# Search rounds ahead of the first expert, and weight conversions ahead of their gather, in an attention, feed-forward and routed-experts kernel

## The chip, the core and the metric

The kernel runs on one core of a Trainium2 chip. The metric is the device time of one execution in microseconds (us); lower is better. The core's engines work side by side, each through its own list of instructions in order: PE multiplies matrices, DVE, ACT and POOL work on elements, SP issues most transfers, and POOL also issues the transfers whose rows are picked by an index.

## The reference

Three parts follow one another: causal attention with a memory term over 4 x 8 heads, 576 positions of 64; a feed-forward layer with squared ReLU over the 2304 resulting tokens of 512 numbers; and a layer of eight experts, with 288 tokens each, cut here to what matters:

```python
def _moe2_ref(x, w_gate, w1, w2):
    N, D = x.shape
    E = w_gate.shape[1]
    cap = N // E
    logits = x @ w_gate
    flat = logits.flatten()
    order = np.argsort(-flat)
    ...
    for idx in order:
        tok, e = (int(idx) // E, int(idx) % E)
        if assigned[tok] >= 0 or counts[e] >= cap:
            continue
        assigned[tok] = e
        counts[e] += 1
    ...
    for e in range(E):
        mask = assigned == e
        h = np.maximum(x[mask] @ w1[e], 0.0)
        out[mask] = h @ w2[e]
```

All token and expert pairs are taken in order of falling score, and each pair whose token is free and whose expert has room is joined. Each expert then multiplies its own 288 tokens by its two weight matrices.

## The kernel before

Attention and the feed-forward layer take the first 740 us and are the same in both kernels. The change lies in the last stage, class `Moe`.

**Routing.** The greedy join is done in phases (`phase`). A phase finds the expert that fills next, by a search for a threshold: `search` is called twice, on the upper and the lower 16 bits of the scores, and does three rounds each. A round is a comparison on DVE (`cmp`), 18 small counting matmuls on PE (`rs<-hot,cmp`), a comparison on DVE (`fl`), one matmul that spreads the answer (`rs<-fl,jo`), and a sum on DVE (`nb`). So a phase has six rounds, then a count (`gm`) and a prefix sum over tokens (`ab`, `prefix`), after which the expert's number is known (`number`, tile `ei`). `lists` then turns the members into three lists of 96 token numbers (18 small matmuls `rs<-rhs,oh`, tile `idx`).

**An expert's data.** `load` brings its weights in four transfers of 1 MB into `wraw` (three buffers), issued by SP once the number is known. `gather` brings its 288 rows by three transfers that POOL issues (`xg`). `convert` splits each loaded part into a high and a low half (`wsp`, six buffers): two activations on ACT, then two subtractions on POOL. In the kernel before, the conversion stands inside `lists`, behind the gather.

**An expert's products.** `head` transposes the gathered rows on PE and splits them (`xs`); `hidden` does 8 blocks of 12 products (`ph<-xs,wsp`) with results to `hs`; `output` 4 blocks of 24 (`ph<-hs,wsp`) with results to `yt`; `tail` transposes back and POOL stores the rows. An expert has 192 products.

**The order on PE** is written out by `run`: every yield of `mlps` is one product or transpose, every yield of `routes` one step of the routing, and the number that the step yields says how many products go by before the next step. `LEAD` is the number of routing steps that stand ahead of the first expert (two steps a round). A factor of 0.75 cuts short waits while fewer experts are ready than `AHEAD` allows. `EARLY` is the number of experts whose list is finished at once, not in pieces beside the next phase's search.

**The order on the other engines** (ACT, DVE, POOL, SP) is chosen by the framework's scheduler when the kernel is built, from the dependences and its own model of durations; `issue_after` adds an order between two engines' instructions. In the built program each engine keeps that order strictly.

Of the kernel before, what the change touches and what calls it, by code (L numbers as in the profile page):

```python
# [383 lines left out]
def run(work):  # L384

    while True:
        try:
            next(work)
        except StopIteration as e:
            return e.value  # L390


class Ffn:
# [123 lines left out]
    def later(self, gpool, beside, turn):  # L517
# [12 lines left out]
        def hide(n, c):  # L530
            last = n == len(steps) - 1 and c != PASSES[-1][0]
            G[n][c] = run(self.hidden(xs[n], c, self.gb if last else gpool))

        get(0)
        for n, (p, i) in enumerate(steps):
# [41 lines left out]
            for d in range(KD):  # L577
                py = self.p2x.tile([128, 512], F32, name="py")[:, 0:TW]
                run(self.output(py, G[n], cs, d))
                nc.vector.tensor_tensor(y[:, d], py, y[:, d], op=OP.add)  # L580
            if not final:
                nc.sync.dma_start(self.yp_d[1][i].rearrange("(k p) t -> p k t", p=128), self.Y.pop(i))
            else:
                after = [lambda i=i: run(self.logits(i)), lambda i=i: run(self.rows(i))]
# [82 lines left out]
NE = 8  # L667
# [7 lines left out]
NEVER = 1 << 30  # L675
CUTS = (2, 2, 2, 2)
ON_DVE = ()
LEAD = 6
GAPS = (60, 12, 12, 15, 12, 12, 12, 18, 48, 6)
AHEAD = 3  # L680
EARLY = 2


class Moe:
# [116 lines left out]
    def t18(self, nm, dt=F32):  # L801
        return self.rt.tile([128, NTT], dt, name=nm)
# [149 lines left out]
    def lists(self, i, raws):  # L952

        nc, V, two, t18 = self.nc, self.nc.vector, self.rt, self.t18
        yield "v"
        j, r, pos, rb, jh = t18("j"), t18("r"), self.pos, self.rb, self.jh
        V.tensor_scalar(j, pos, float(CW), None, op0=OP.is_ge)
        V.scalar_tensor_tensor(j, pos, float(2 * CW), j, op0=OP.is_ge, op1=OP.add)
        V.scalar_tensor_tensor(r, j, -float(CW), pos, op0=OP.mult, op1=OP.add)
        V.scalar_tensor_tensor(rb, r, 1.0, self.mem, op0=OP.add, op1=OP.mult)  # L960
        V.tensor_tensor(jh, j[:, :, None].to_broadcast([128, NTT, 3]),
                        self.j3p[:, None, :].to_broadcast([128, NTT, 3]), op=OP.is_equal)
        rhs = two.tile([128, NTT, 3, 2], BF16, name="rhs")
        V.tensor_tensor(rhs, jh[:, :, :, None].to_broadcast([128, NTT, 3, 2]),
                        self.tp[:, :, None, :].to_broadcast([128, NTT, 3, 2]), op=OP.mult)
        oh = two.tile([128, NTT, CW], BF16, name="oh")
        n = NTT // CUTS[3]
        for t0 in range(0, NTT, n):
            yield "v"
            V.tensor_tensor(oh[:, t0:t0 + n], rb[:, t0:t0 + n, None].to_broadcast([128, n, CW]),  # L970
                            self.slot[:, None, :].to_broadcast([128, n, CW]), op=OP.is_equal)
        yield "p"
        ps = self.p1.tile([CW, 3, 2], F32, name="rs")
        for t in range(NTT):
            nc.tensor.matmul(ps.rearrange("p a b -> p (a b)"), oh[:, t], rhs[:, t].rearrange("p a b -> p (a b)"),
                             start=(t == 0), stop=(t == NTT - 1))
        yield "v"
        V.tensor_reduce(self.idf[0:CW], ps, axis=mybir.AxisListType.X, op=OP.add)
        idx = self.ri.tile([CW, 3], I32, name="idx")
        V.tensor_copy(idx, self.idf[0:CW])  # L980
        self.ready.append((self.split[i], idx, self.gather(idx)))
        with self.tc.issue_after(self.got):
            self.convert(i, raws if i else raws[:1])
        if i == 0:
            self.raws = raws[1:]

    def number(self):
# [4 lines left out]
    def routes(self):  # L992

        self.beside = self.wants = None
        for i in range(NE):
            if i < NE - 1:
                yield from self.phase()
            else:
                yield from self.finish()
                yield from self.rest()  # L1000
            er = self.number()
            if i == 0:
                self.settle()
            raws, self.split[i] = self.load(er), []
            self.beside = self.lists(i, raws)
            self.wants = next(self.beside)
            if i < EARLY or i == NE - 1:
                yield from self.finish()

    def finish(self):  # L1010
# [93 lines left out]
    def mlps(self, routes):  # L1104

        yield from self.head(0, range(KD))
        with self.tc.issue_after(self.last):
            self.convert(0, self.raws)
        for i in range(NE):
            for f in range(KE):  # L1110
                yield from self.hidden(i, f)
                if 1 <= f <= 3 and i:
                    yield from self.tail(i - 1, [f - 1])
            for d in range(KD - 1):
                yield from self.output(i, d)
            work = self.output(i, KD - 1)
            if i + 1 < NE:
                while len(self.ready) <= i + 1:
                    next(routes, None)
                for k in range(0, KD, 2):  # L1120
                    yield from self.head(i + 1, [k, k + 1])
                    for _ in range(KE * 3 // 2 if k == 0 else 0):
                        next(work)
                        yield
            yield from work
            self.done = i + 1
        yield from self.tail(NE - 1, range(3))

    def run(self, close, other, settle):

        self.settle = settle
        with self.tc.manual_schedule(engines={mybir.EngineType.PE}):
            routes, wait = self.routes(), 0
            owed = 0
            close()
            while not self.ready:
                owed += min(0.6 * next(routes, 0), 24)
                while owed > 0:
                    owed -= next(other, NEVER)
            for _ in range(LEAD):  # L1140
                wait = next(routes)
            for _ in self.mlps(routes):
                wait -= 1
                if wait <= 0 and len(self.ready) <= self.done + AHEAD:
                    wait = next(routes, NEVER)
                    if len(self.ready) < self.done + AHEAD and wait <= 15:
                        wait *= 0.75


@with_exitstack  # L1150
# [126 lines left out]
```

## Time and profile before

| | us |
|---|---|
| median of 3 runs | 1064.56 |
| the three runs | 1064.21 to 1068.12 |
| the profiled execution | 1064.33 |
| its span in the profile | 1062.6 |
| PE busy (91% of the span) | 970.3 |
| DVE, ACT, POOL busy | 666.0, 554.7, 526.0 |

The span runs from the first to the last instruction; the execution's own time has 1.7 us around it. A busy share is an average over the whole kernel. What the change is worth is to be read from the stage of the experts alone, and there from what PE waits for, and from the clock that PE is granted (PEclk, 1.00 is 2.4 GHz and 0.50 is 1.2 GHz).

### The profile page before, as it was taken

The numbers are of one execution on the slowest core, as the hardware profiler recorded it, in microseconds if no ns is written. First come the engines' busy times: TensorE is split into PE (matmuls) and PEld (weight loads), VectorE is DVE, ScalarE is ACT, GpSimd is POOL, SyncE is SP. The second block draws the span as 40 slices with busy tenths as digits, with TensorE's granted clock in tenths as the row PEclk, the third lists the DMA queues.
The fourth block names the chain that finished last, engine by engine and source line by source line (L and its number), as shares of the span: only waits on it lengthen the run. The fifth ranks groups of instructions, "written<-read, shape, count | busy, mean of one in ns | idle before, by whom it ended". The sixth has DMA issues, their size and how long they took to land.

```text
span 1062.6 us, 19791 instructions
## 1 busy us (share of the span) xinstructions
PE 970.3 (91%) x7017; PEld 886.8 (83%) x7017; DVE 666.0 (63%) x1966; ACT 554.7 (52%) x1370; POOL 526.0 (50%) x503
## 2 busy tenths in 40 slices
PE   4677799999999988999999999998789989999996
PEld 3555588989898988999999999875688888889996
DVE  7998878888888737256428932336557567773110
ACT  6776878888888745344323333521442334344531
POOL 3665666566656525345212111211763637878841
PEclk9767899999999999999999999999689689999999
DMA  6453455464636277679573333002452345445501
GB/s 149 121 152 101 113 148 157 94 171 110 179 75 166 63 231 234 209 252 312 184 265 107 119 120 120 30 21 72 150 181 91 114 156 181 156 145 180 192 26 30
DMA packets 150723, 150.75 MB, mean 142 GB/s; under 512 B 71640, under 2 KB 122840, under 8 KB 150496
## 3 DMA queue, kind: packets, MB, share of 16 engines
q1 hardware_dynamic: 147552, 140.05, 43.2%
q0 software_dynamic: 3072, 9.44, 2.9%
q8 instruction: 55, 0.90, 0.3%
q14 instruction: 44, 0.36, 0.1%
HBM read 111.69 MB, written 37.77 MB: 141 GB/s over the span
## 4 chain that ended last, share of the span: by engine, by line
PE 61%; DVE 13%; issue 9%; ACT 7%; DMA 6%; POOL 3%; SPq 2%; POOLq 0%; ACTq 0%; DVEq 0%
PE ph L1053 12%; PE ph L44 7%; PE ph L45 6%; PE ph L46 6%; PE py L44 4%; PE py L45 4%; PE py L46 4%; PE ps L312 3%; ACT P L240 2%; PE ps L217 2%; PE ps L271 2%; DMA xg<-y_d,idx 2%; PE rs L832 2%; DMA wraw<-in_moe_w_dram 2%; DVE ptb L26 1%
## 5 line engine op out<-in xcount | busy, mean ns | idle before, releaser
L477 POOL TENSOR_TENSOR gf<-r 128x384 f32<-128x384 f32 (+1 forms) x108 | 87.0, 806 | 206.6 <-ACT r L475 198.3
L1037 POOL TENSOR_TENSOR wsp<-wraw,wsp 128x1024 fp32r<-128x1024 f32 x64 | 150.5, 2383 | 11.9 <-ACT wsp L1035 11.6
L1053 PE MATMUL ph<-hs,wsp 128*128 128x288 f32 x768 | 124.9, 317 | 0.9 <-DVE hs L1077 0.9
L1053 PE MATMUL ph<-xs,wsp 128*128 128x288 f32 x768 | 121.5, 308 | 0.0
L26 DVE TENSOR_TENSOR gs<-gf,gs 128x384 fp32r<-128x384 f32 (+1 forms) x108 | 63.7, 590 | 91.5 <-ACT gs L25 90.9
L1053 PEld LDWEIGHTS ph<-hs,wsp 128*128 128x128 f32 x768 | 112.1, 201 | 2.8 <-DVE hs L1077 1.6
L246 POOL TENSOR_SCALAR P<-P,R,og 128x128 f32<-128x128 f32 (+2 forms) x144 | 94.7, 671 | 34.1 <-DVE R L244 14.7
L1053 PEld LDWEIGHTS ph<-xs,wsp 128*128 128x128 f32 x768 | 107.8, 193 | 1.2 <-issue 0.5
L475 ACT ACTIVATE r<-ph 128x384 f32<-128x384 f32 (+1 forms) x108 | 48.6, 450 | 75.6 <-PE ph L46 74.4
L1035 ACT ACTIVATE wsp<-wraw 128x1024 fp32r<-128x1024 f32 x64 | 64.1, 1051 | 44.1 <-DMA wraw<-in_moe_w_dram 28.6
L240 ACT ACTIVATE P<-P,R 128x128 f32<-128x128 f32 (+2 forms) x144 | 83.2, 579 | 6.8 <-POOL P L246 2.7
L25 ACT ACTIVATE gs<-gf 128x384 fp32r<-128x384 f32 (+1 forms) x108 | 52.5, 486 | 56.2 <-POOL gf L477 48.0
L44 PE MATMUL ph<-xt,win 128*128 128x384 f32 x240 | 81.3, 339 | 0.0
L45 PE MATMUL ph<-xt,win 128*128 128x384 f32 x240 | 80.9, 337 | 0.0
L46 PE MATMUL ph<-xt,win 128*128 128x384 f32 x240 | 80.7, 336 | 0.0
L271 PE MATMUL ps<-ident,P 128*128 128x128 f32 x320 | 62.2, 302 | 12.0 <-POOL P L246 4.9
L44 PE MATMUL ph<-xs,win 128*128 128x288 f32 x192 | 63.5, 331 | 3.9 <-ACT yo L514 2.6
L45 PE MATMUL py<-gs,wout 128*128 128x384 f32 x192 | 64.6, 337 | 0.0
L217 PE MATMUL ps<-kt,qt 64*128 64x128 f32 (+3 forms) x384 | 55.8, 386 | 9.4 <-DVE kt L26 3.5
L26 DVE TENSOR_TENSOR ptb<-ps,ptb 128x256 fp32r<-128x256 f32 (+3 forms) x128 | 59.6, 467 | 7.3 <-ACT ptb L25 5.7
L46 PE MATMUL py<-gs,wout 128*128 128x384 f32 x192 | 63.9, 336 | 0.0
L44 PE MATMUL py<-gs,wout 128*128 128x384 f32 x192 | 63.4, 338 | 0.0
(259 smaller groups left out, 2610.6 us busy)
## 6 DMA issues: line engine op xcount, KB each, us to landing
wraw<-in_moe_w_dram SPq DMA_DIRECT2D x32, 1024.0 KB, 5.4
xt<-xs_d SPq DMA_DIRECT2D x12, 1536.0 KB, 7.7
x_d<-xo SPq DMA_DIRECT2D x32, 288.0 KB, 3.9
xf<-x_d SPq DMA_DIRECT2D x32, 288.0 KB, 3.5
xs_d<-xs SPq DMA_DIRECT2D x8, 1152.0 KB, 5.9
raw<-in_moe_w_in_dram SPq DMA_DIRECT2D x16, 512.0 KB, 4.2
raw<-in_moe_w_out_dram SPq DMA_DIRECT2D x16, 512.0 KB, 4.4
yp<-yo SPq DMA_DIRECT2D x32, 144.0 KB, 3.6
```

Source lines behind the costliest of these rows:

```text
L26: (eng or nc.vector).tensor_tensor(lo, src, hi.bitcast(F32), op=OP.subtract)
L44: nc.tensor.matmul(out, lhi, rhi, start=start, stop=False)
L45: nc.tensor.matmul(out, lhi, rlo, start=False, stop=False)
L46: nc.tensor.matmul(out, llo, rhi, start=False, stop=stop)
L217: nc.tensor.matmul(ps[j][:, 0:w], qt[r0, a, qs], kt[r0, b, 0:w], start=i == 0, stop=i == 2)
L240: nc.scalar.activation(pw, pw, AF.Exp, bias=R[:, 0, u:u + 1], scale=-1.0, accum_out=R[:, 1, u:u + 1])
L246: nc.gpsimd.tensor_scalar(PP[n][w], PP[n][w], R[:, 2, w:w + 1], og9[:, hp, w:w + 1], op0=OP.mult, op1=OP.mult)
L271: nc.tensor.transpose(tr[:, 128 * i:128 * i + 128], P[:, 128 * i:128 * i + 128], ident)
L477: nc.gpsimd.tensor_tensor(gf, r, r, op=OP.mult)
L1035: nc.scalar.activation(w[:, 0, hs], raw[:, hs], AF.Copy)
L1037: eng.tensor_tensor(w[:, 1, hs], raw[:, hs], w[:, 0, hs].bitcast(F32), op=OP.subtract)
L1053: nc.tensor.matmul(out, l[a], r[b], start=i + p == 0, stop=i == n - 1 and p == 2)
```

## The change

Four edits go together. `LEAD` is 12, so that six rounds of the second phase's search stand ahead of expert 0, not three. The weights of experts 1 to 7 are converted where they are loaded, ahead of their list and gather. Expert 1's list is no longer finished at once. The factor of 0.75 is gone.

```diff
--- before.py
+++ after.py
@@ -675,10 +675,9 @@
 NEVER = 1 << 30
 CUTS = (2, 2, 2, 2)
 ON_DVE = ()
-LEAD = 6
+LEAD = 12
 GAPS = (60, 12, 12, 15, 12, 12, 12, 18, 48, 6)
 AHEAD = 3
-EARLY = 2
 
 
 class Moe:
@@ -979,9 +978,9 @@
         idx = self.ri.tile([CW, 3], I32, name="idx")
         V.tensor_copy(idx, self.idf[0:CW])
         self.ready.append((self.split[i], idx, self.gather(idx)))
-        with self.tc.issue_after(self.got):
-            self.convert(i, raws if i else raws[:1])
         if i == 0:
+            with self.tc.issue_after(self.got):
+                self.convert(i, raws[:1])
             self.raws = raws[1:]
 
     def number(self):
@@ -1002,9 +1001,11 @@
             if i == 0:
                 self.settle()
             raws, self.split[i] = self.load(er), []
+            if i:
+                self.convert(i, raws)
             self.beside = self.lists(i, raws)
             self.wants = next(self.beside)
-            if i < EARLY or i == NE - 1:
+            if i in (0, NE - 1):
                 yield from self.finish()
 
     def finish(self):
@@ -1143,8 +1144,6 @@
                 wait -= 1
                 if wait <= 0 and len(self.ready) <= self.done + AHEAD:
                     wait = next(routes, NEVER)
-                    if len(self.ready) < self.done + AHEAD and wait <= 15:
-                        wait *= 0.75
 
 
 @with_exitstack
```

Where it moves instructions. First POOL, from the gather of expert 0 on (`xg` is a gather, `wsp` a conversion, two for each of an expert's four parts, `out_dram` a store). The kernel before:

```order
L1044 DMA xg<-y_d,idx 96x512 x3
L1037 TENSOR_TENSOR wsp<-wraw,wsp 128x1024 x8
L1044 DMA xg<-y_d,idx 96x512 x3
L1037 TENSOR_TENSOR wsp<-wraw,wsp 128x1024 x8
L1098 DMA out_dram<-yo,idx 2304x512 x3
L1044 DMA xg<-y_d,idx 96x512 x3
L1037 TENSOR_TENSOR wsp<-wraw,wsp 128x1024 x8
```

The changed kernel:

```order
L1045 DMA xg<-y_d,idx 96x512 x3
L1038 TENSOR_TENSOR wsp<-wraw,wsp 128x1024 x14
L1045 DMA xg<-y_d,idx 96x512 x3
L1038 TENSOR_TENSOR wsp<-wraw,wsp 128x1024 x2
L1099 DMA out_dram<-yo,idx 2304x512 x3
L1038 TENSOR_TENSOR wsp<-wraw,wsp 128x1024 x6
L1045 DMA xg<-y_d,idx 96x512 x3
```

Expert 1's gather, the second one, stood behind the eight conversions of expert 0; it now stands behind these and six of its own. Expert 2's stands behind six of its own too.

Then PE, at the end of the last round ahead of expert 0 (`tr<-ident,xg` are the transposes of expert 0, `ph<-xs,wsp` its products). The kernel before:

```order
L832 MATMUL rs<-hot,cmp 32x8
L837 LDWEIGHTS jo_1_94
L837 MATMUL rs<-fl,jo_1_94 128x8
L1065 MATMUL tr<-ident,xg 128x96 x12
L1053 MATMUL ph<-xs,wsp 128x288 x3
L832 LDWEIGHTS cmp
L832 MATMUL rs<-hot,cmp 64x8
```

The changed kernel:

```order
L831 MATMUL rs<-hot,cmp 32x8
L836 LDWEIGHTS jo_1_111
L836 MATMUL rs<-fl,jo_1_111 128x8
L1066 MATMUL tr<-ident,xg 128x96 x12
L883 LDWEIGHTS ones
L883 MATMUL rs<-gm,ones 128x288
L1054 MATMUL ph<-xs,wsp 128x288 x18
```

Before, a round follows after three products; now the search is over ahead of the transposes (its last round is the one of `jo_1_111`), and the count `gm` follows them.

Last ACT, from the last block of expert 0's hidden layer before, and from its fifth in the changed kernel (`hs` reads a block of the hidden layer, `wsp` are the conversions of expert 1's weights, `yt` reads a block of the output). The kernel before:

```order
L1076 ACTIVATE hs_9856<-ph 128x288
L1035 ACTIVATE wsp<-wraw 128x1024 x2
L1086 ACTIVATE yt<-ph 128x288
L1035 ACTIVATE wsp<-wraw 128x1024 x2
L1086 ACTIVATE yt<-ph 128x288
L1035 ACTIVATE wsp<-wraw 128x1024 x2
L1086 ACTIVATE yt<-ph 128x288
L25 ACTIVATE xs<-tr 128x288 x2
L1035 ACTIVATE wsp<-wraw 128x1024 x2
```

The changed kernel:

```order
L1077 ACTIVATE hs_9848<-ph 128x288
L1036 ACTIVATE wsp<-wraw 128x1024 x2
L1077 ACTIVATE hs_9864<-ph 128x288
L1077 ACTIVATE hs_9910<-ph 128x288
L1036 ACTIVATE wsp<-wraw 128x1024 x2
L1077 ACTIVATE hs_9947<-ph 128x288
L1036 ACTIVATE wsp<-wraw 128x1024 x2
L1087 ACTIVATE yt<-ph 128x288
L1036 ACTIVATE wsp<-wraw 128x1024 x2
L1087 ACTIVATE yt<-ph 128x288 x2
```

The first conversions of expert 1 stood behind all eight `hs`; they now stand ahead of the sixth.

## Rows read from the trace of the kernel before

**Rows 1.** The profile's page: its first line.
```profile
span 1062.6 us, 19791 instructions
```

**Rows 2.** Stretches, experts 0 to 5: length; engines' busy time (count); PEclk; DMA share; GB/s.
```profile
755.80:799.40 43.60, 40.33 (x342) 36.45 (x340) 23.01 (x88) 19.89 (x31) 32.77 (x16) 0.85 0.33 112
799.40:847.20 47.80, 45.57 (x409) 40.79 (x410) 30.47 (x114) 14.25 (x25) 20.49 (x14) 0.82 0.35 114
847.20:889.60 42.40, 39.09 (x356) 36.20 (x356) 28.04 (x115) 17.39 (x29) 25.28 (x15) 0.92 0.38 128
889.60:930.70 41.10, 38.58 (x391) 34.82 (x391) 32.16 (x124) 17.49 (x29) 29.96 (x17) 1.00 0.56 194
930.70:969.20 38.50, 37.04 (x354) 34.80 (x353) 24.69 (x94) 15.36 (x27) 28.75 (x18) 0.96 0.54 172
969.20:997.40 28.20, 28.20 (x218) 27.97 (x218) 4.93 (x12) 14.56 (x25) 23.76 (x15) 1.00 0.57 180
```

**Rows 3.** Timeline of PE in experts 1 and 2: one round; one list.
```profile
822.97 0.18 PE L837 MATMUL rs<-fl,jo 64*128 64x8 bf16 x1
823.07 1.47 PE L1053 MATMUL ph<-hs,wsp 128*128 128x288 f32 x9
824.47 0.61 PE L832 MATMUL rs<-hot,cmp 128*32 128x8 bf16 x18
825.01 0.93 PE L1053 MATMUL ph<-hs,wsp 128*128 128x288 f32 x5
...
870.55 0.93 PE L975 MATMUL rs<-rhs,oh 128*96 128x6 bf16 x18 [1.51 <-DVE nb L841]
```

**Rows 4.** Timeline of DVE ahead of expert 0: where four rounds begin.
```profile
744.62 1.41 DVE L823 SCALAR_TENSOR_TENSOR cmp<-bank,jt 128x576 bf16<-128x576 int32 x2
...
747.39 0.94 DVE L823 SCALAR_TENSOR_TENSOR cmp<-bank,nb,jt 128x288 bf16<-128x288 int32 x2
...
749.44 0.94 DVE L823 SCALAR_TENSOR_TENSOR cmp<-bank,nb,jt 128x288 bf16<-128x288 int32 x2
...
751.77 1.42 DVE L823 SCALAR_TENSOR_TENSOR cmp<-bank,jt 128x576 bf16<-128x576 f32 x2
```

**Rows 5.** Timeline of PE: expert 0's transposes wait, then its first products.
```profile
753.48 0.90 PE L1065 MATMUL tr<-ident,xg 96*128 96x96 f32 x4 [1.72 <-DMA xg<-y_d,idx]
...
755.83 1.07 PE L1053 MATMUL ph<-xs,wsp 128*128 128x288 f32 x3
```

**Rows 6.** Timeline of POOL: conversions of expert 0, gathers of experts 1 and 2.
```profile
757.59 14.09 POOL L1037 TENSOR_TENSOR wsp<-wraw,wsp 128x1024 fp32r<-128x1024 f32 x6 [6.48 <-ACT wsp L1035]
...
782.53 0.92 POOL L1044 DMA_INDIRECT xg<-y_d,idx  x1 [0.30 <-issue]
...
831.61 0.94 POOL L1044 DMA_INDIRECT xg<-y_d,idx  x1 [18.82 <-DVE idx L980]
...
834.09 0.92 POOL L1044 DMA_INDIRECT xg<-y_d,idx  x1 [0.30 <-issue]
```

**Rows 7.** Timeline of PE: the transposes that follow the last gathered third.
```profile
789.83 0.42 PE L1065 MATMUL tr<-ident,xg 96*128 96x96 f32 x1 [0.53 <-DMA xg<-y_d,idx]
...
837.12 0.90 PE L1065 MATMUL tr<-ident,xg 96*128 96x96 f32 x4 [0.62 <-DMA xg<-y_d,idx]
```

**Rows 8.** Timelines of PE, DVE, SP, ACT: from prefix to conversion, expert 2.
```profile
812.68 0.18 PE L938 MATMUL rs<-ab,tri 128*128 128x36 bf16 x1
...
816.27 0.15 DVE L989 TENSOR_SCALAR ei<-bank 128x1 int32<-128x1 f32 x1
...
817.24 1.60 SPq L1025 DMA_DIRECT2D wraw<-in_moe_w_dram  x3
...
822.41 2.01 ACT L1035 ACTIVATE wsp<-wraw 128x1024 fp32r<-128x1024 f32 x2 [0.94 <-DMA wraw<-in_moe_w_dram]
```

**Rows 9.** Two stretches of expert 1, columns as in the stretches above.
```profile
829.00:832.00 3.00, 2.81 (x28) 2.81 (x28) 2.13 (x7) 0.79 (x1) 0.39 (x1) 0.73 0.00 0
...
844.00:847.00 3.00, 3.00 (x15) 2.71 (x13) 1.37 (x7) 0.00 (x0) 3.00 (x3) 0.50 0.08 25
```

## The prediction

> **What bounds the kernel now.** I read the page first, then the stretches by expert, then the timelines where PE stands or its clock is low, last POOL's and ACT's queues. The sum is made against the profiled execution, 1064.3 us, which is a span of 1062.6 [rows 1] and 1.7 around it; it lies 0.2 below the median of the runs shown. Everything ahead of the experts is the same, so only the last 310 us count.
>
> In expert 5 nothing is searched any more: 28.2 us at full clock, PE busy throughout [rows 2]. That is the price of an expert on PE, for 192 products and 24 transposes, so about 0.134 us a product if a transpose takes 0.1. Experts 0 to 4 take 43.6, 47.8, 42.4, 41.1 and 38.5 us [rows 2]. How much of that is routing? From one spreading matmul to the products after the next count, 2.04 us pass with nine products in them, then five products take 0.93 [rows 3]: 2.97 us for 14 products that cost 1.88 alone, so a round costs PE 1.1 us. A list costs 0.93 and a wait for DVE, 1.51 in a bad case [rows 3]; I take 1.2. Count and prefix I take at 0.5 an expert, an estimate. I counted the routing in the built order of before: 6, 9, 6, 7 and 5 rounds in experts 0 to 4, one list in each and three in expert 4. What an expert should take, and what it loses beyond that:
>
> - expert 0 (no tail, 1.3 less): 26.9 + 6.6 + 1.7 = 35.2, loses 8.4
> - expert 1: 28.2 + 9.9 + 1.7 = 39.8, loses 8.0
> - expert 2: 28.2 + 6.6 + 1.7 = 36.5, loses 5.9
> - expert 3: 28.2 + 7.7 + 1.7 = 37.6, loses 3.5
> - expert 4: 28.2 + 5.5 + 3.6 + 0.5 = 37.8, loses 0.7
>
> So 26.5 us are lost, 22.3 of them in the first three experts, and their granted clock is 0.85, 0.82 and 0.92 where the others have 1.00 and 0.96 [rows 2]. That loss, not the count of rounds, is what the change can touch. In expert 1 the clock falls during 829 to 832 (a mean of 0.73 puts the fall at 830.4) and is at half at 844 to 847 [rows 9], and in it stands a wait for gathered rows [rows 7]: the list came late, POOL stood idle 18.8 us for it and issued the gather at 831.6 [rows 6].
>
> **The change, part by part.**
>
> *Three rounds move ahead of expert 0.* There they hide behind nothing but the gather. On DVE a round of 64 steps takes 2.77 us, one of 32 steps 2.05, and the fourth begins at 751.8 [rows 4]; so the sixth ends at 751.8 + 2.77 + 2 x 2.05 = 758.6. Before, the transposes waited for the gather until 753.5 and the first product came 2.35 later [rows 5]. Now the gather has landed and the transposes start whole, which I put at 0.6 more: first product at 758.6 + 0.6 + 2.35 = 761.5, so **5.7 us later**. Bounds: 4 (rounds run as fast as the spacing allows while DVE splits wait) to 7 (all of the three rounds, 6.9).
>
> *Expert 1's gather stands behind twelve conversions.* Six conversions take 14.1 us on POOL and began at 757.6 [rows 6], after expert 0's last transposes; now 757.6 + 5.7 = 763.3. Six of expert 1 follow, their weights loaded meanwhile: 763.3 + 28.2 = 791.5. Three gathers are issued over 2.5 us [rows 6], and the last third lands 3.0 later when no load is in flight (issued 834.1, used 837.1), but 7.3 later when loads run beside it (782.5 to 789.8) [rows 6, 7]. Expert 1's last load is queued behind its first conversion and should have landed by then, so I take 3.0: 791.5 + 0.2 + 2.5 + 3.0 = 797.2; the other end is 801.5. PE gets there by 789.8 + 5.7 + 2.2 for two rounds more = 797.7 had it not waited before, so it waits 2 us or less more than it did. From the last third to expert 1 before took 799.4 - 789.8 = 9.6 with three rounds in it; one remains: 7.4. **Expert 1 starts at 804.6, which is 5.2 us late.**
>
> *Expert 1 gets six rounds for nine, and its list stands late in the first half.* Expert 2's number is known early: its prefix is now a few products into expert 1. From there: 3.6 us on DVE to the number, 1.0 to the load, 5.2 to the conversion on ACT [rows 8], 1 for its first half, 14.1 for six conversions, then 2.7 and 3.0 for the gather [rows 6, 7]: 30.6 us. PE reaches the transposes of expert 2 about 5 us before the end of an expert of 38.6 us, so 33 us after that prefix. The gather is in time by 2 us; that is all the margin there is. Then the late gather and the low clock after it go. I do not let the whole loss vanish: where the clock was nearly full, experts 3 and 4 still lost 3.5 and 0.7, mean 2.1. So expert 1 takes 36.5 + 2.1 = 38.6, **-9.2**.
>
> *Experts 2 to 5.* Expert 2 keeps six rounds: 38.6, **-3.8**. Expert 3 gets eight for seven: 28.2 + 8.8 + 1.7 + 2.1 = 40.8, **-0.3**. Expert 4 gets four for five and two lists for three; its 0.7 stays: 36.2, **-2.3**. Expert 5 gets a list: **+1.2**. Experts 6 and 7 are unchanged.
>
> *Conversions ahead on ACT* cost nothing in the sum: they are the same 64 activations. But an activation that waits for its load holds the `hs` behind it, DVE waits for that `hs` and PE for DVE. Four PSUM buffers of results, 12 products each, cover about 6 us of it. That is in the 2.1 us. *The dropped factor* sets 6 and 12 products between steps for 5 and 9, which gives each round's chain more cover; below zero it can cost only rounds that slip into later experts, and these are counted above.
>
> Sum: 5.2 - 9.2 - 3.8 - 0.3 - 2.3 + 1.2 = -9.2, so 1064.3 - 9.2 = **1055.1**.
>
> One rule of the Trainium skill sizes the largest term otherwise. By the rows expert 1 loses 8.0 us in all, its waits for rows included. The Trainium skill, "TensorE: Matmul & The Clock Gate", section "Terms", prices a throttled stretch at its length times one less the granted share. By that the 17 us from 830.4 to 847.2 would cost 8.4 without the waits, and expert 1 would come out some 2 us shorter than I say. The measured loss is the smaller, and I go by it.
>
> **The rivals.**
>
> *The late gather comes back at each expert (slower).* The chain of 30.6 us from prefix to gathered rows is now in front of PE for experts 2 and 3 too, since on POOL the gather cannot start before six conversions. If it runs over by more than the 2 us of margin, PE waits, the clock falls and an expert loses 8.4, as expert 0 does, not 2.1. For it: loads that meet a gather take 7.3 us where 3.0 is the rule [rows 6, 7]; ACT is more often held. Against it: expert 3's and 4's prefixes come half an expert earlier. With experts 1, 2 and 3 hit: 1055.1 + 3 x 6.3 = 1074; from two on it is no gain.
>
> *The clock falls anyway (no change).* It fell in expert 1 at 830.4, ahead of the wait for rows, with PE between rounds and a list [rows 9]. The rounds stay. If one such stretch stays, some 7 us are back: 1062.
>
> *Nearly all loss goes.* If experts 1 to 3 lose 0.7 as expert 4 does: 1055.1 - 3 x 1.4 = 1051; with the page's price of the low clock, 1049.
>
> That the change would not do what it says is excluded by the built order, where the rounds and conversions stand as described.
>
> **How the numbers follow.** A difference of 0.5%, 5.3 us, is about what a measurement of this kernel can tell from no change. Forecast 0.48, its own range 1050 to 1060 (bounds of the lead-in and of the gather's landing); nearly all goes 0.12; the clock falls anyway 0.24; late gathers 0.16. The first two are faster: 0.60; same 0.24; slower 0.16. The range reaches from the best case, 1047, to 1069, where one or two late gathers end; beyond lie most of the slower case and little below.
>
> **What would show it.** First product of expert 0 near 761.5; expert 1's gather issued near 792 with twelve conversions ahead of it; expert 1 starting near 805 and taking under 40 us with PEclk 1.00 in its second half; expert 2 starting near 843, ahead of 847.2. Wrong if PE waits for gathered rows at the end of expert 1 or 2, or if ACT's conversions wait for loads while `hs` stands behind them and the lists slip; then experts 1 to 3 take over 42 us each.

## The result and the profile after

Four executions of the changed kernel took 1050.7 to 1053.66 us, median 1052.03; four of the kernel before 1064.21 to 1071.71, median 1066.34. The ratio is 0.9856, with a 95% interval of 0.9827 to 0.9886: faster by 1.4%. The forecast was 1055.1 in a range of 1047 to 1069, and faster was its likeliest case. The profiled execution took 1052.92 us, 11.4 below that of before; the medians lie 14.3 apart. In a second comparison, with other runs of the kernel before, the same kernel had a ratio of 0.9884 (0.984 to 0.9928), where 0.983 to 0.989 was expected.

The first line of the changed kernel's page, to lay beside [rows 1]:

```profile
span 1051.2 us, 19788 instructions
```

The stretches of experts 0 to 5 in the changed kernel, with the columns of [rows 2]:

```profile
761.40:804.80 43.40, 39.76 (x341) 36.57 (x340) 25.95 (x101) 19.56 (x31) 35.66 (x17) 0.87 0.33 112
804.80:845.20 40.40, 37.45 (x356) 34.56 (x355) 26.77 (x107) 15.71 (x27) 24.38 (x14) 0.96 0.39 135
845.20:881.90 36.70, 35.63 (x353) 33.12 (x352) 25.89 (x103) 15.27 (x27) 24.53 (x14) 1.00 0.43 150
881.90:921.30 39.40, 37.70 (x391) 34.51 (x389) 28.90 (x110) 16.41 (x28) 25.29 (x15) 1.00 0.55 197
921.30:956.70 35.40, 34.75 (x337) 32.72 (x335) 25.50 (x96) 15.14 (x28) 27.14 (x18) 1.00 0.52 171
956.70:986.00 29.30, 29.30 (x237) 28.96 (x236) 5.85 (x15) 15.23 (x29) 24.61 (x15) 1.00 0.62 203
```

Expert 0 begins 5.6 us later than before and takes as long. Experts 1 and 2 take 7.4 and 5.7 us less, experts 3 and 4 take 1.7 and 3.1 less, and expert 5 takes 1.1 more. The granted clock of experts 1 and 2 rose from 0.82 and 0.92 to 0.96 and 1.00.

The two tables also show where the time went. Experts 0 to 5 together became 17.0 us shorter. Only 2.8 of this is time in which PE stood idle; 14.2 is PE's busy time, for the same products and three rounds fewer. The three rounds are worth 3.3 at the prediction's price, so most of the gain is the same work done at the higher clock.

Where does the search end, and when is expert 1's gather issued? The timeline of PE in the changed kernel, which answers to [rows 5, 7]:

```profile
758.45 0.16 PE L836 MATMUL rs<-fl,jo 32*128 32x8 bf16 x1 [0.24 <-DVE fl L833]
758.55 1.21 PE L1066 MATMUL tr<-ident,xg 96*128 96x96 f32 x6
...
761.38 4.70 PE L1054 MATMUL ph<-xs,wsp 128*128 128x288 f32 x18
...
794.55 0.31 PE L1066 MATMUL tr<-ident,xg 96*128 96x96 f32 x1 [1.40 <-DMA xg<-y_d,idx]
795.54 0.30 PE L1066 MATMUL tr<-ident,xg 96*128 96x96 f32 x1 [0.69 <-DMA xg<-y_d,idx]
796.90 0.42 PE L1066 MATMUL tr<-ident,xg 96*128 96x96 f32 x1 [1.06 <-DMA xg<-y_d,idx]
...
839.90 0.66 PE L1066 MATMUL tr<-ident,xg 96*128 96x96 f32 x6
```

The transposes of expert 0 no longer wait for a gather; they follow the sixth round at once. Those of expert 1 wait three times, 3.15 us in all. Those of expert 2, at 839.90, do not wait. POOL's timeline, which answers to [rows 6], says why:

```profile
762.98 28.22 POOL L1038 TENSOR_TENSOR wsp<-wraw,wsp 128x1024 fp32r<-128x1024 f32 x12 [11.64 <-ACT wsp L1036]
791.33 0.92 POOL L1045 DMA_INDIRECT xg<-y_d,idx  x1
...
832.93 0.94 POOL L1045 DMA_INDIRECT xg<-y_d,idx  x1
...
835.40 0.92 POOL L1045 DMA_INDIRECT xg<-y_d,idx  x1 [0.30 <-issue]
```

Twelve conversions stand ahead of expert 1's gather, without a gap. DVE's timeline has the two lists:

```profile
785.54 0.16 DVE L979 CAST idx<-bank 96x3 int32<-96x3 f32 x1
...
828.05 0.15 DVE L979 CAST idx<-bank 96x3 int32<-96x3 f32 x1
```

So expert 1's list was ready 5.8 us before its gather was issued, and expert 2's 4.9 us. The first delay reached PE, the second did not.

The rest of expert 1's loss is a chain that begins with a load. ACT's timeline, DVE's and PE's in the changed kernel:

```profile
817.60 2.01 ACT L1036 ACTIVATE wsp<-wraw 128x1024 fp32r<-128x1024 f32 x2 [4.14 <-DMA wraw<-in_moe_w_dram]
819.51 0.39 ACT L1077 ACTIVATE hs<-ph 128x288 fp32r<-128x288 f32 x1
```

```profile
819.93 0.46 DVE L1078 SCALAR_TENSOR_TENSOR hs<-ph,hs 128x288 fp32r<-128x288 f32 x1 [1.56 <-ACT hs L1077]
820.31 0.14 DVE L833 TENSOR_TENSOR fl<-rs,room 32x8 bf16<-32x8 f32 x1
```

```profile
820.50 0.16 PE L836 MATMUL rs<-fl,jo 32*128 32x8 bf16 x1 [1.50 <-DVE fl L833]
```

ACT stood 4.14 us for the load of expert 2's part, `hs` stood behind that conversion, DVE's `fl` behind `hs`, and PE waited 1.50 us for `fl`. The granted clock of the three microseconds from 820 on is 0.60.

### The profile page after: what moved, and what is told of

It is laid out like the page before. It is cut to its first block, busy times and chain, and to the rows that moved or that the text cites. A ratio compares the mean times of both kernels' runs of the same rounds, so it can differ in the third digit from the quotient of the medians.

```text
span 1051.2 us, 19788 instructions
## 1 busy us (share of the span) xinstructions
PE 959.6 (91%) x7017; PEld 879.5 (84%) x7017; DVE 666.5 (63%) x1966; ACT 553.2 (53%) x1370; POOL 528.1 (50%) x503
## 4 chain that ended last, share of the span: by engine, by line
PE 62%; DVE 13%; ACT 9%; issue 7%; DMA 4%; POOL 3%; SPq 2%; POOLq 0%; ACTq 0%; DVEq 0%
PE ph L1054 12%; PE ph L44 7%; PE ph L45 6%; PE ph L46 6%; PE py L44 4%; PE py L45 4%; PE py L46 4%; ACT P L240 3%; POOL wsp L1038 3%; PE ps L312 3%; PE ps L217 2%; PE rs L831 2%; PE ps L271 2%; DMA wraw<-in_moe_w_dram 1%; DVE ptb L26 1%
## 5 line engine op out<-in xcount | busy, mean ns | idle before, releaser
L1054 PE MATMUL ph<-hs,wsp 128*128 128x288 f32 x768 | 115.9, 304 | 0.0
L1054 PEld LDWEIGHTS ph<-hs,wsp 128*128 128x128 f32 x768 | 105.7, 191 | 0.9 <-DVE hs L1078 0.4
L45 PE MATMUL py<-gs,wout 128*128 128x384 f32 x192 | 64.6, 337 | 0.0
L46 PE MATMUL py<-gs,wout 128*128 128x384 f32 x192 | 63.9, 336 | 0.0
L228 DVE CUSTOM_DVE_ANT_0 P<-ps,maskw 128x128 f32<-128x128 f32 (+3 forms) x128 | 58.6, 483 | 7.6 <-PE ps L135 4.1
```

Of the source, the lines that this page charges most:

```text
L45: nc.tensor.matmul(out, lhi, rlo, start=False, stop=False)
L46: nc.tensor.matmul(out, llo, rhi, start=False, stop=stop)
L1054: nc.tensor.matmul(out, l[a], r[b], start=i + p == 0, stop=i == n - 1 and p == 2)
```

## The experiments

The part ahead of the experts took 738.9 to 746.3 us in the fourteen profiles of this study, as read from the first matmul of expert 0's list on PE, though the work there is the same. So beside the ratio I give the **stage**: from that matmul to the end of the span. It was 322.6 us before (739.99 to 1062.6) and 311.0 in the changed kernel (740.18 to 1051.2). Each ratio is against runs of the kernel before on the same chip. There the kernel before had a median of 1066.34 for the change itself, 1075.03 for kernels 1 to 4, 1071.73 for 7, 8, 9 and the second run of 5, and 1067.54 for the rest. A stage is read from one profiled execution, and the kernel before was profiled only once, beside the change. So stages of different groups compare badly, and the ratios are the fairer comparison.

| kernel | ratio, 95% interval | stage, us |
|---|---|---|
| the change | 0.9856 (0.9827 to 0.9886) | 311.0 |
| the change, once more | 0.9884 (0.984 to 0.9928) | 310.9 |
| 1. change, conversions behind the gather | 0.9827 (0.9752 to 0.9901) | 310.8 |
| 2. change, expert 1's alone behind it | 0.9916 (0.9877 to 0.9955) | 320.8 |
| 3. change, LEAD 6 | 1.0065 (1.0024 to 1.0106) | 338.1 |
| 4. change, factor kept | 0.9883 (0.9849 to 0.9917) | 319.1 |
| 5. before, LEAD 12 | 0.985 (0.9802 to 0.9897) | 306.3 |
| 5. before, LEAD 12, once more | 0.983 (0.9787 to 0.9873) | 309.4 |
| 6. before, conversions ahead | 1.0107 (1.0043 to 1.017) | 333.6 |
| 7. before, LEAD 12, factor dropped | 0.988 (0.9824 to 0.9936) | 316.6 |
| 8. before, LEAD 12, EARLY 1 | 0.9834 (0.9777 to 0.9891) | 314.7 |
| 9. before, LEAD 8 | 0.9835 (0.9793 to 0.9878) | 315.1 |
| 10. change, extra matmuls | 0.9888 (0.9848 to 0.9928) | 309.6 |

**1. The changed kernel with all conversions behind their gather again.**

```diff
@@ the end of lists
-        if i == 0:
-            with self.tc.issue_after(self.got):
-                self.convert(i, raws[:1])
+        with self.tc.issue_after(self.got):
+            self.convert(i, raws if i else raws[:1])
@@ routes
-            if i:
-                self.convert(i, raws)
```

> The changed kernel with all conversions of weights back behind their gather, the other three edits kept. Theory A (the early conversions cost, the gain comes from the routing standing earlier): expert 1's gather no longer waits for six conversions, it is issued near 785 instead of 791.3, PE does not wait for its rows and the clock stays up at the end of expert 0, so expert 1 starts near 799 instead of 804.8, and the whole is 4 to 7 us below the changed kernel, near 1047. Theory B (the early conversions are the gain, since POOL no longer idles for a gather): it loses most of the 12 us, 1059 or more.

The ratio is 0.9827 and the stage 310.8, as the changed kernel's. Inside it, expert 0 shrank by 6.6 us: expert 1's gather was issued at 787.20, 24.2 us after expert 0's start, where the changed kernel took 29.9 (791.33 less 761.4), and expert 1 started at 799.8. So theory A holds for expert 0 and fails for the whole, and theory B falls. The stretches of experts 0, 3 and 5:

```profile
763.00:799.80 36.80, 36.33 (x342) 33.87 (x341) 25.45 (x99) 17.54 (x29) 26.14 (x13) 0.95 0.39 132
...
876.40:917.80 41.40, 37.80 (x390) 34.42 (x389) 28.53 (x110) 16.52 (x27) 27.09 (x16) 1.00 0.52 180
...
954.10:987.00 32.90, 30.92 (x235) 30.34 (x235) 5.76 (x15) 15.06 (x28) 25.84 (x16) 0.95 0.61 203
```

PE waits for no gathered row in this kernel, so the twelve conversions are what delayed expert 1's gather. But experts 3 and 5 give back 2.0 and 3.6 us. In expert 5 a conversion now comes in the middle of the products. What ACT waited for ahead of it the profile gives only as `remote`. ACT's timeline and PE's:

```profile
971.68 2.01 ACT L1034 ACTIVATE wsp<-wraw 128x1024 fp32r<-128x1024 f32 x2 [3.51 <-remote]
973.59 0.39 ACT L1075 ACTIVATE hs<-ph 128x288 fp32r<-128x288 f32 x1
```

```profile
974.03 6.25 PE L1052 MATMUL ph<-hs,wsp 128*128 128x288 f32 x31 [1.89 <-ACT hs L1075]
```

So where the conversions stand moves a loss from one expert to others. It is not what made the change faster.

**2. The changed kernel with expert 1's conversions alone behind the gather.**

```diff
-        if i == 0:
+        if i < 2:
             with self.tc.issue_after(self.got):
-                self.convert(i, raws[:1])
+                self.convert(i, raws if i else raws[:1])
@@ routes
-            if i:
+            if i > 1:
                 self.convert(i, raws)
```

> The changed kernel with the conversions of expert 1 alone back behind its gather. Theory A: expert 1's gather near 785, expert 1 starts near 799, the whole 4 to 7 us below the changed kernel, near 1047. Theory B (early conversions are the gain): about the changed kernel's time, 1050 to 1054, since experts 2 to 7 keep them. If this one and the one with all conversions late come out alike, the early conversions of experts 2 to 7 are worth nothing.

Expert 0 took 38.8 us, but experts 2 to 4 took 40.2, 42.0 and 42.3, and the stage 320.8. The gain in expert 0 came as in the first experiment; the sum did not. PE's wait for `fl` from 757 to 1055 in this kernel (us in total, times, longest):

```profile
PE rs L836 <- DVE fl L833: 10.1, 11, 2.9
```

In the changed kernel the same view has:

```profile
PE rs L836 <- DVE fl L833: 2.8, 4, 1.5
```

The wait for `fl` rose from 2.8 to 10.1 us. ACT's timeline and PE's, in expert 2 of this kernel, show one of these waits:

```profile
849.67 2.00 ACT L1037 ACTIVATE wsp<-wraw 128x1024 fp32r<-128x1024 f32 x2 [3.50 <-DMA wraw<-in_moe_w_dram]
```

```profile
852.58 0.16 PE L836 MATMUL rs<-fl,jo 64*128 64x8 bf16 x1 [2.15 <-DVE fl L833]
```

ACT waits 3.50 us for a load and PE, some 3 us later, 2.15 for `fl`. It is the chain of the changed kernel's expert 1 at another place. The longest wait, 2.94 us in expert 4, follows 3.55 us of ACT for which the profile shows no load. And the ratio, 0.9916, is not clear of the changed kernel's second, 0.9884, so a cost of this edit in the whole is not shown.

**3. The changed kernel with LEAD 6.**

```diff
-LEAD = 12
+LEAD = 6
```

> The changed kernel with three rounds ahead of expert 0 as before. Theory A: the first product comes 5.7 us sooner, near 755.8, but two more rounds fall into expert 0 and expert 1's number, loads, conversions and gather come later, so expert 1 starts no sooner than 805 to 809 and the whole is 3 to 6 us slower than the changed kernel, 1055 to 1058. Rival (the lead-in is a plain cost): 4 to 6 us faster, near 1047.

Far worse than either theory: 0.65% slower than the kernel before, with a stage of 338.1. Its stretches of experts 0 and 1, then PE's timeline and POOL's:

```profile
757.20:815.00 57.80, 44.10 (x379) 39.95 (x378) 27.84 (x104) 20.14 (x31) 35.46 (x17) 0.74 0.25 86
815.00:860.50 45.50, 40.50 (x373) 36.68 (x372) 26.15 (x100) 16.04 (x27) 24.37 (x14) 0.89 0.36 120
```

```profile
802.20 0.42 PE L1066 MATMUL tr<-ident,xg 96*128 96x96 f32 x1 [11.44 <-DMA xg<-y_d,idx]
803.45 0.42 PE L1066 MATMUL tr<-ident,xg 96*128 96x96 f32 x1 [0.83 <-DMA xg<-y_d,idx]
804.69 0.42 PE L1066 MATMUL tr<-ident,xg 96*128 96x96 f32 x1 [0.82 <-DMA xg<-y_d,idx]
```

```profile
785.04 13.95 POOL L1038 TENSOR_TENSOR wsp<-wraw,wsp 128x1024 fp32r<-128x1024 f32 x6 [12.02 <-ACT wsp L1036]
799.14 0.92 POOL L1045 DMA_INDIRECT xg<-y_d,idx  x1 [0.16 <-issue]
```

DVE wrote this list at 791.81, in the middle of six conversions of expert 1, which began only at 785.04 because its number came late: 20.6 us after expert 0's start (777.80 less 757.2), and 6.4 in the changed kernel (767.80 less 761.4). The gather stood 7.3 us behind them and PE waited 13.1 us for rows. This is the prediction's rival of the late gather, at expert 1.

**4. The changed kernel with the factor of 0.75 kept.**

```diff
                     wait = next(routes, NEVER)
+                    if len(self.ready) < self.done + AHEAD and wait <= 15:
+                        wait *= 0.75
```

> The changed kernel with the factor of 0.75 back, so that 5 and 9 products stand between the steps of a round instead of 6 and 12. Theory A (the lost time of experts 1 and 2 came from late lists and gathers): within 4 us of the changed kernel, 1049 to 1056, granted clock of expert 1 above 0.95. Theory C (the denser products between rounds are what keep the clock up): the clock falls in expert 1 as before, its mean below 0.9, and the whole is 6 us or more slower, 1058 or more.

The ratio is 0.9883, within the intervals of the changed kernel's two. The clock of expert 1 was 0.92, between the two theories. The profiled stage is 8.1 us longer; expert 2, with nine rounds and two lists, took 46.7 us at a clock of 0.96. By the ratio the factor makes no difference that can be measured, and the stage of a single profile is not enough to say that it does.

**5. The kernel before with LEAD 12 and nothing else.** It ran twice.

```diff
-LEAD = 6
+LEAD = 12
```

> The kernel before, with six search rounds ahead of expert 0 and nothing else of the change. Theory A (the rounds taken out of experts 0 and 1 are the gain; where the conversions stand only moves a loss about): expert 0 shortens from 43.6 to about 37 us since the list and gather of expert 1 now come ahead of need, expert 1 takes about 40 for 47.8, experts 3 and 4 get the rounds of the dropped factor; with 5.7 us of later start the whole is 4 to 16 us faster, ratio 0.985 to 0.996. Theory B (rounds ahead and conversions ahead pay only together, since POOL is idle only when the conversions stand ahead): the gather of expert 2 is as late as before and experts 1 and 2 lose as before; ratio 0.997 or more.

> The kernel before with LEAD = 12 alone, a second time. The stage of the experts is taken here as the time from the first matmul of expert 0's list on PE to the end of the span, since the part ahead of it took 740 to 746 us in the profiles so far. It was 322.6 in the kernel before, 311.0 and 310.9 in the changed kernel, 306.3 with LEAD = 12 alone. If the 306.3 belongs to the kernel and not to one execution: 305 to 308, and the whole 0.2 to 0.6% below the changed kernel's, ratio 0.980 to 0.988.

One number gives all of the gain: 0.985 and 0.983. Its first three stretches in the first profile:

```profile
767.50:804.00 36.50, 35.74 (x342) 32.96 (x339) 23.87 (x89) 19.41 (x32) 34.10 (x17) 0.97 0.40 133
804.00:843.20 39.20, 36.73 (x355) 33.53 (x355) 28.93 (x120) 14.54 (x25) 18.86 (x12) 1.00 0.41 139
843.20:885.80 42.60, 40.16 (x391) 36.11 (x390) 31.40 (x120) 18.65 (x32) 31.47 (x18) 0.96 0.54 179
```

Experts 0 and 1 take 7.1 and 8.6 us less than before [rows 2]. Over experts 0 to 2 PE's busy time fell by 12.4 us and its idle time by 3.1, with two rounds fewer in them, so here too most of it is the clock. POOL's timeline shows that expert 1's gather follows expert 0's conversions with no gap, and no transpose of PE waits for rows:

```profile
769.14 14.19 POOL L1037 TENSOR_TENSOR wsp<-wraw,wsp 128x1024 fp32r<-128x1024 f32 x6 [11.71 <-ACT wsp L1035]
783.47 0.92 POOL L1044 DMA_INDIRECT xg<-y_d,idx  x1
```

Theory A holds and theory B falls. The second profile, on another chip, had a stage of 309.4, outside the 305 to 308 that I expected, with 45.3 us for expert 2 at a clock of 0.89 instead of 42.6 at 0.96. So a stage of one kernel can differ by 3 us between executions, and that this kernel beats the changed one, as I expected of the second run, is not shown: the intervals overlap.

**6. The kernel before with conversions ahead and nothing else.**

```diff
-        with self.tc.issue_after(self.got):
-            self.convert(i, raws if i else raws[:1])
         if i == 0:
+            with self.tc.issue_after(self.got):
+                self.convert(i, raws[:1])
@@ routes
+            if i:
+                self.convert(i, raws)
```

> The kernel before, with the conversions of experts 1 to 7 ahead of their gather and nothing else of the change. Theory A: nothing gained, since the rounds stay in experts 0 and 1; ACT's conversions stand ahead of hs more often and wait for loads; expert 1 takes 46 us or more, ratio 0.998 to 1.010. Theory B: the 18.8 us in which POOL stood idle ahead of the second expert's gather now hold six conversions, so something is gained even without the rounds; ratio 0.990 to 0.997.

Slower by 1.1%, just over the upper end of theory A; theory B falls. Expert 1 took 53.9 us. Expert 2's list was written at 838.48; POOL's timeline and PE's:

```profile
830.75 14.00 POOL L1039 TENSOR_TENSOR wsp<-wraw,wsp 128x1024 fp32r<-128x1024 f32 x6 [10.71 <-ACT wsp L1037]
844.90 0.94 POOL L1046 DMA_INDIRECT xg<-y_d,idx  x1
```

```profile
848.05 0.42 PE L1067 MATMUL tr<-ident,xg 96*128 96x96 f32 x1 [7.65 <-DMA xg<-y_d,idx]
```

POOL's idle 18.8 us ahead of this gather [rows 6] could hold six conversions, but their loads come so late that they fill its end: the list then waits 6.4 us, and PE 7.65 and more.

**7 and 8. LEAD 12 with one of the two other edits.** One drops the two lines of the factor, the other sets `EARLY = 1`, both in the kernel before with `LEAD = 12`.

```diff
-LEAD = 6
+LEAD = 12
@@ 7 alone
-                    if len(self.ready) < self.done + AHEAD and wait <= 15:
-                        wait *= 0.75
@@ 8 alone
-EARLY = 2
+EARLY = 1
```

> LEAD = 12 and the dropped factor, nothing else of the change. LEAD alone gave a stage of 306.3, and with the factor dropped and EARLY = 1 besides it was 310.8 (late conversions). Theory E (the dropped factor costs, since it pushes rounds into experts 4 and 5 and the last list into expert 5): stage 309 to 312, experts 4 and 5 together 66 or more for 60.9. Theory F (the split list of expert 1 costs): stage 305 to 308.

> LEAD = 12 and EARLY = 1, nothing else of the change. Theory E (the dropped factor costs): stage 305 to 308. Theory F (EARLY = 1 costs, since expert 1's list is no longer finished at once and its gather slips): stage 309 to 312, expert 1's gather issued over 2 us later than 783.5 less 767.5 = 16.0 us after the first product, or expert 2 with nine rounds over 44 us.

Each theory finds its sign in its own kernel and is contradicted by the other's stage. In 7, experts 4 and 5 together took 70.6 us. In 8, expert 1's gather was issued 24.2 us after expert 0's start (789.97 less 765.8), and expert 2, with nine rounds, took 48.9 us at a clock of 0.86. In 7, expert 2, with six rounds, took 44.5 at 0.88. The stages, 316.6 and 314.7, are longer than the 309.4 of LEAD alone on the same chip. But the ratios, 0.988 and 0.9834, cannot be told from its 0.983. The kernel of experiment 1 is LEAD 12 with both edits, and it had 0.9827. So no cost or gain of the two edits beside LEAD 12 is shown, singly or together.

**9. The kernel before with LEAD 8.**

```diff
-LEAD = 6
+LEAD = 8
```

> The kernel before with LEAD = 8: four rounds ahead of expert 0. Theory A (what pays is that expert 1's list and gather come ahead of need; six rounds give more than is needed): PE's margin on the gather of expert 1 was about 10 us with six rounds, two rounds among products take 3 to 5 us of it, so no wait for rows; the first product comes 4.1 us earlier against the list (17.1 for 21.2), expert 0 takes 38 to 41 for 36.5: stage 304 to 308, as LEAD = 12 or a little less. Rival (the gain needs the whole search out of the way: the rounds that stay make PE wait and the clock fall in expert 0): expert 0 takes 42 or more and the stage 311 or more.

Expert 0 took 37.3 us, a little less than theory A's 38 to 41, without a wait for rows, so the rival falls there; the only such wait, 0.3 us, came at expert 2's transposes. The stage, 315.1, is the rival's all the same: expert 2 took 44.1 at a clock of 0.85 and expert 3, with nine rounds, 46.4. In expert 2 PE waited for no rows. Its clock was at half from 852 to 864, after six microseconds in which PE was busy for 4.45, with a wait of 1.5 for `fl` of a search round. The ratio is 0.9835. So by the whole time four rounds ahead do what six do, as far as it can be measured.

**10. The changed kernel with 31 extra matmuls ahead of expert 0.**

```diff
+            pd = self.p2.tile([128, 512], F32, name="tr")
+            wide = self.ones[:, None, :].to_broadcast([128, 4, 128])
-            for _ in range(LEAD):
+            for step in range(LEAD):
+                for _ in range(16 if step == 0 else (0, 3)[step % 2 == 0]):
+                    self.nc.tensor.matmul(pd.rearrange("p (a b) -> p a b", a=4), self.ones, wide, start=True, stop=True)
                 wait = next(routes)
```

> The changed kernel with 31 extra matmuls (ones by ones, result not used) on PE in the waits ahead of expert 0, so that PE is not idle there. Theory C (the clock that is granted at half from about 743 to 766 follows from PE's idle time ahead of expert 0 and costs there): the clock stays at 1.00 through the rounds, the six counts of 18 matmuls take about 0.5 us for 0.83 to 1.3, expert 0's transposes and first 18 products take half (12 transposes 1.2 for 2.4, products 2.4 for 4.7): first product of expert 0 at 757 to 759 for 761.4, expert 1 some 3 to 6 us earlier, the whole 3 to 6 us below the changed kernel. Theory D (the clock falls for another reason, the load of 16 DMA engines or DVE, or the extra matmuls hold up the rounds): the clock stays at 0.50 ahead of expert 0 and the first product comes as late or up to 5 us later; the whole is 0 to 5 us above the changed kernel.

Theory C falls: the first product came 22.4 us after the first matmul of the list (768.67 less 746.28), and 21.2 in the changed kernel. Theory D fits the times, but the clock did not stay at half. PE's timeline has the sixteen matmuls of the first wait, and three after each of two rounds:

```profile
747.67 5.30 PE L1145 MATMUL tr<-ones 128*128 128x512 bf16 x16
...
753.97 0.82 PE L1145 MATMUL tr<-ones 128*128 128x512 bf16 x3
...
758.03 1.43 PE L1145 MATMUL tr<-ones 128*128 128x512 bf16 x3
```

The stretches of that time, columns as before:

```profile
744.00:751.00 7.00, 4.70 (x29) 2.19 (x28) 5.43 (x16) 0.00 (x0) 1.60 (x2) 0.78 0.65 212
751.00:758.00 7.00, 6.04 (x72) 3.10 (x70) 4.38 (x15) 2.00 (x2) 6.05 (x4) 0.98 1.05 344
758.00:769.00 11.00, 9.71 (x81) 5.68 (x81) 6.68 (x24) 1.39 (x4) 0.00 (x0) 0.50 0.33 108
```

The clock rose to full for some seven microseconds (three matmuls in 0.82) and fell to half again (1.43), with PE busy 6.04 of 7 and 9.71 of 11 us. The stage is 309.6, for 310.9 of the changed kernel on the same chip, and the ratio the same. The low clock ahead of expert 0 is not settled by keeping PE busy in this way; what would hold it up stays open.

## Why the prediction was right, step by step

*The lead-in.* Forecast 5.7 us later with the first product at 761.5; it came at 761.38. The rounds on DVE and the transposes behind them were priced rightly.

*Expert 1's gather behind twelve conversions.* Forecast: issued near 791.5, last third used at 797.2, expert 1 at 804.6. Measured: 791.33, 796.90, 804.82. Experiment 1 shows that the conversions are the cause: without them expert 0 takes 36.8 us for 43.4.

*Expert 1.* Forecast 38.6 us, -9.2; 40.4 in the profile. It came out just over the 40 that was to be the sign. The mechanism held: expert 2's gather was issued at 832.93 to 835.40 and PE did not wait for it. With the 3.0 us of [rows 6, 7] to land, its last third was there 1.5 us ahead of the transposes at 839.90, where 2 was forecast. The clock in the stretch where it fell before [rows 9] is 1.00. The rest is the stall behind the load at 817.6, which the prediction had named and counted into its 2.1 us, and the low clock after it. The second profile of the same kernel, experts 1 to 4:

```profile
805.50:844.00 38.50, 35.97 (x354) 33.16 (x354) 26.43 (x107) 15.61 (x27) 24.38 (x14) 1.00 0.40 141
844.00:882.10 38.10, 37.03 (x354) 34.37 (x353) 26.02 (x103) 15.47 (x27) 24.50 (x14) 0.96 0.44 144
882.10:921.80 39.70, 38.73 (x390) 35.48 (x389) 28.81 (x110) 16.80 (x28) 25.44 (x15) 0.96 0.55 197
921.80:957.20 35.40, 34.76 (x337) 32.74 (x335) 25.49 (x96) 15.03 (x27) 26.95 (x18) 1.00 0.52 172
```

Expert 1 took 38.5 here at full clock, and experts 2 and 3 had 0.96. So the difference of 1.8 lies within what one expert varies between executions. With the two levels, a mean of 0.96 means that 3.2 of the 40.4 us stood at half, an estimate. The Trainium skill, "TensorE: Matmul & The Clock Gate", section "Terms", prices a throttled time at its length times one less the granted share: 3.2 x 0.5 = 1.6, an estimate by that page. The two profiles agree with it here: PE was busy in expert 1 for 37.45 us in the one and 35.97 in the other, 1.5 less.

*Experts 2 to 4.* Forecast 38.6, 40.8 and 36.2; measured 36.7, 39.4 and 35.4. This is the step of the sum that was mis-sized: I let a loss of 2.1 us stay in experts 1 to 3, the mean of two experts of before. By the same reckoning of rounds and lists expert 1 lost 3.9 (40.4 less 36.5), expert 2 lost 0.2 (36.7 less 36.5), and experts 3 and 4 together 0.6 (74.8 less 74.2): 4.7 in all, where 7.0 was forecast. In the second profile the four lost 4.5, otherwise shared out: 2.0, 1.6 and 0.9. So the loss that stays was set too large, and which expert bears it differs between executions. The trace has one round on the other side of the border between experts 3 and 4 than the prediction counted: 8 and 4 rounds before, 7 and 5 after. Their sum, and so the forecast, is the same.

*Expert 5.* Forecast +1.2, measured +1.1. The sum in the profile is -11.4 for a forecast -9.2. Experts 2 to 4 came out 4.1 us better than forecast and expert 1 1.8 worse; that these partly cancel is luck.

*What carried the gain.* The prediction put it on the search: the rounds leave expert 1, its list and the next gather come ahead of need, and the clock stays up. Experiment 5 shows with that edit alone that the rounds carry the gain, that the list and gather come ahead of need, and that the clock is higher. At the end of expert 0 the step from the wait for rows to the clock is seen too: with the wait the clock fell to half at 797, and without it, in experiments 1 and 5, it stayed at 1.00. But late rows are not the whole cause of the low clock: in experiment 9 it fell in expert 2 after a wait for a search round. Why it held where it did is not shown in full. The prediction gave the conversions no gain; experiments 1 and 6 bear that out, and in 6 they cost 1.1%.

*The rivals.* The late gather is real: it is what experiments 3 and 6 show, with 13.1 us of waits at expert 1's transposes in the one, and 7.65 and more at expert 2's in the other. The change escapes it because expert 1's number is known early: its prefix comes 4.6 us after expert 0's first product (765.96 less 761.38), and with LEAD 6 it came 16.3 us after it (773.53 less 757.2). The clock that falls anyway was seen, but it cost some 2 us in one or two of experts 1 to 3, not 7. Nearly all loss gone would have been 1051, with 2.8 us lost in experts 1 to 4. The profiled 1052.9 lies between it and the forecast, as the 4.7 and 4.5 us lost do.

## What to carry to other kernels

Find the chain that must end before the next tile's data can be asked for, and take its first link out of the stage where it competes: three more short rounds that nothing hides cost 5.6 us once, and two tiles later 13 were back. Moving work ahead on an in-order engine is paid where a gather or a read-out stands behind it; look at what waits in that queue, and at how late the moved work's own loads land. Undo each part of a bundled change by itself before crediting it: here one of four edits gave the whole gain, one was harmful without it, and the others could not be told from nothing.

## What was not expected of the hardware

The stage ahead of the experts, with the same work, took 738.9 to 746.3 us in single executions, so a difference of a few microseconds in the whole says little without the stage's own time. The granted clock stood at half for 11 us in which extra matmuls, counts and products kept PE busy for 9.71, after 7 us at full level with PE busy for 6.04; why it fell is not known. And the clock fell to half in an expert of experiment 9 in which PE waited for no rows, after one wait of 1.5 us for a search round; why it fell there is not known either.
